# One query against 8192 keys, sixteen heads: another signal for the K loads, fixed transpose addresses, another end

## The chip, the cores and the metric

The kernel runs on one core of a Trainium2 chip. Its metric is the time of one execution on the device, in microseconds, the median over several runs. The core has a matrix engine (TensorE, PE in the profile), three engines for element work (VectorE, DVE; ScalarE, ACT; GpSimd, POOL), a fifth that only issues transfers (SyncE, SP), and 16 DMA engines that bring data from memory to the on-chip buffers. Each engine runs its own instruction list; they meet through counters (semaphores) that one engine raises and another waits for.

## The reference, cut

```python
B, H, Sq, Sk, D = 1, 16, 1, 8192, 256          # q, k, v in bf16

def reference(q, k, v):
    scale = q.shape[-1] ** -0.5
    scores = jnp.einsum("bhqd,bhkd->bhqk", q, k) * scale
    p = _softmax(scores, axis=-1)
    return jnp.einsum("bhqk,bhkd->bhqd", p, v)
```

For each of 16 heads one query row is multiplied with 8192 keys, the scores go through a softmax, and the weights sum up 8192 rows of V. K and V of a head are 4 MB each, so 134 MB are read for 8 KB of output.

## The kernel before

A head's 8192 rows are laid out as 128 partitions of 64 rows each: partition p holds rows 64p to 64p + 63, and "column" j is the j-th row of every partition, 256 numbers in each. `kbuf` and `vbuf` each hold two heads; even heads use the first half, odd heads the second (the parity of the head).

**Loads.** SyncE issues every load in the order of a list, `stream`, built at the top. It begins K0 (in three pieces), K1, the first half of V0, K2, the rest of V0, half of V1, K3, the rest of V1, and then K of head h+2 and V of head h in turn. All go through one queue. Before K of head h (from head 2 on) SyncE waits for the counter `m`, before V of head h for `pr`: the buffer's former user must be done. V of the last two heads is cut into 4 and 9 pieces, and nothing of K comes behind K15. GpSimd waits for each landing and raises `kc` (by eights of columns) or `vc` (by pairs of columns); this is `POOLq L179` and `L181` in the profile.

**Scores.** VectorE computes the first 48 columns of a head, one instruction each (L238: multiply with the query, sum into one column of `S`), in three runs of 16 (`NC` = 3, the loop variable is c); each half run raises `kd` (preset to 2, 6 per head). TensorE computes the last 16 columns: four groups of four columns are transposed into `tp` (`ktrans`, L302, eight transposes a group, each with an address that the engine's sequencer works out from the head), ScalarE copies each group to `KT` (L429), and TensorE multiplies (L316); ScalarE copies the 16 results to `S` and raises `sc`.

**Softmax.** The largest score is found in steps that travel with the next head: four columns into head h+1 VectorE takes the maximum of head h over each partition (`largest`, L214, raises `m`), TensorE transposes that (L284, `mT`), VectorE reduces it after column 16 (`xmax`, L205, raises `g`), TensorE spreads it to all partitions (L288), ScalarE makes the exponentials `E` (even columns in its first half, odd ones in its second) and their sum.

**Values.** TensorE takes V two columns at a time (L374): one matmul of 33 weight columns against 512 numbers, of which row 0 with the first 256 (the even column) and row 32 with the last 256 (the odd column) are used; a head is 32 such pairs after a zeroing matmul (L369). It works on head h-2 while the scores of head h are made: its list for one turn is scores of h, values of h-2, sum of h-1. ScalarE then brings row 32, scaled, to `part` (`other`, L451), and VectorE adds row 0, scaled (`final_of`, L217), into `o_sb`. The last head ends differently: its last eight columns are in a branch of their own, the last four of them go singly into another bank (`TAIL`, L402), and VectorE does two operations, `part` and then `o_sb`. ScalarE then stores all 16 heads, 8 KB in one row (L486).

The counters start from presets, which GpSimd gives at the start from `AHEAD`.

Of the kernel before, what the change touches and what calls it, by code (L numbers as in the profile page):

```python
# [12 lines left out]
GRP = 4  # L13
CH = 8
RUN = 16
PL = 4
ROWS = 33
K_FIRST = (16, 32)
V_SPLIT = {
# [3 lines left out]
    14: (0, 16, 32, 48),  # L23
    15: (0, 16, 32, 40, 48, 52, 56, 60, 62),
}
AHEAD = {"vc": 64, "sc": 1, "sp": 2, "m": 1, "fin": 4, "rc": 3, "l": 2, "qs": 2, "pr": 3, "pt": 3, "kd": 2}


def bass_standalone__mha_softmax__decode_kernel(nc: bass.Bass, q: bass.AP, k: bass.AP, v: bass.AP, out: bass.AP):
# [10 lines left out]
    NC = JD // RUN  # L40
    VU = J // 2
    LAST = H - 1
    TAIL = (LAST + 1) % 2 * 512
    dt = k.dtype


# [27 lines left out]
    with contextlib.ExitStack() as ctx:  # L74
# [60 lines left out]
        for name in ("l", "rc", "pr", "pt", "ps", "pv", "fin", "kd", "ldq", "out"):  # L135
            sem(name)
        for _, _, _, _, name, _ in stream:
            sem(name)
# [4 lines left out]
        @(lambda f: f(nc.sync))  # L143
        def _(sp):
            for kind, h, a, b, name, _ in stream:
                if h >= 2 and a == 0:
                    if kind == "k":
                        sp.wait_ge(sem("m"), h)
                    else:
                        sp.wait_ge(sem("pr"), h + 2)  # L150
                at = (h % 2) * J * D
                sp.dma_start(
                    (kbuf if kind == "k" else vbuf)[:, at + a * D : at + b * D],
                    src(k if kind == "k" else v, h)[:, a * D : b * D],
                ).then_inc(sem(name), 16)
            sp.nop()

        @(lambda f: f(nc.gpsimd))
# [43 lines left out]
        def _(dve):  # L202
# [10 lines left out]
                dve.wait_ge(sem("sc"), h.count(1, 2))  # L213
                dve.tensor_reduce(m[:, :], S[:, ds(h.i * J, J)], AX.X, ALU.max).then_inc(sem("m"), 1)  # L214

            def final(h, bank, to):
                return dve.scalar_tensor_tensor(  # L217
                    out=to,
                    in0=acc[0:1, ds(bank, D)],
                    scalar=recip[0:1, ds(h.i, 1)],  # L220
                    in1=part[0:1, ds(h.i * D, D)],
                    op0=ALU.mult,
                    op1=ALU.add,
                )

            def final_of(h):
                dve.wait_ge(sem("pt"), h.count(1, 4))
                final(h, (h.i % 2) * 512, o_sb[0:1, ds(h.i * D, D)]).then_inc(sem("fin"), 1)

            def turn(h):  # L230
                par = dve.snap(h % 2)
                qh = q_all[:, ds(h * D, D)]
                with dve.Fori(0, NC) as c:
                    dve.wait_ge(sem("kc"), h * KC + c * (RUN // CH) + RUN // CH)
                    for b in range(RUN):
                        if b % (RUN // 2) == 0:
                            dve.wait_ge(sem("kd"), h * (2 * NC) + c * 2 + 1 + b // (RUN // 2))
                        ins = dve.scalar_tensor_tensor(  # L238
                            out=junk[:, b * D : (b + 1) * D],
                            in0=kbuf[:, ds(par * (J * D) + c * (RUN * D) + b * D, D)],  # L240
                            scalar=SCALE,
                            in1=qh,
                            op0=ALU.mult,
                            op1=ALU.mult,
                            accum_out=S[:, ds(h * J + c * RUN + b, 1)],
                        )
                        if b % (RUN // 2) == RUN // 2 - 1:
                            ins.then_inc(sem("kd"), 1)
                        if b == 3:
                            with dve.If(c == 0):  # L250
                                with dve.If(h > 0):
                                    largest(Head(h, 1))
                    with dve.If(c == 0):
                        with dve.If(h > 0):
                            xmax(Head(h, 1))
                    with dve.If(c == 1):  # L256
                        with dve.If(h > 1):
                            recips(Head(h, 2))
                        with dve.If(h > 2):
                            final_of(Head(h, 3))  # L260
                dve.wait_ge(sem("qs"), h // 2 + 4)  # L261

            with dve.Fori(0, 2) as phase:
                with dve.If(phase == 1):
                    dve.wait_ge(sem("qs"), 3)
                    with dve.Fori(0, H) as h:  # L266
                        turn(h)
                    largest(Head(H - 1))
                    recips(Head(H - 2))
                    final_of(Head(H - 3))  # L270
                    xmax(Head(H - 1))
                    recips(Head(H - 1))
                    final_of(Head(H - 2))
                    dve.wait_ge(sem("pt"), H + 3)
                    final(Head(LAST), LAST % 2 * 512, part[0:1, LAST * D : H * D]).then_inc(sem("ps"), 1)
                    dve.wait_ge(sem("ps"), 1)
                    dve.wait_ge(sem("pv"), 1)
                    final(Head(LAST), TAIL, o_sb[0:1, LAST * D : H * D]).then_inc(sem("fin"), 1)

        @(lambda f: f(nc.tensor))  # L280
        def _(pe):
# [14 lines left out]
                    qps[0:ROWS, 0:1], lhsT=lsum[:, 0:1].to_broadcast([P, ROWS]), rhs=ones_col[:, 0:1], start=True, stop=True  # L296
                ).then_inc(sem("l"), 1)

            def ktrans(at, gi):
                for b in range(GRP):  # L300
                    for hf in range(NH):
                        ins = pe.transpose(  # L302
                            tp[gi % 2][:, b * D + hf * P : b * D + (hf + 1) * P],
                            kbuf[:, ds(at + (JD + gi * GRP + b) * D + hf * P, P)],
                            identb[:, :],
                        )
                ins.then_inc(sem("tp"), 1)
# [39 lines left out]
                    ins.then_inc(sem("qp"), 1)  # L347
                pe.wait_ge(sem("cf"), 4)

            def scores(h):  # L350
                now = Head(h)
                at = pe.snap((h % 2) * (J * D))
                pe.wait_ge(sem("kc"), h * KC + KC)
                ktrans(at, 0)
                for gi in range(1, NG):
                    ktrans(at, gi)
                    kscore(now, gi - 1)
                with pe.If(h > 0):
                    transpose_m(Head(h, 1))
                kscore(now, NG - 1)  # L360
                with pe.If(h > 0):
                    bcast(Head(h, 1))

            def values(h):
                o = pe.snap(Head(h, 2).i)
                par = pe.snap(o % 2)
                both = acc[0:ROWS, ds(par * 512, 2 * D)]
                pe.wait_ge(sem("fin"), h + 1)
                pe.matmul(both, lhsT=zero[:, 0:ROWS], rhs=zero[:, :], start=True, stop=False)  # L369

                def pair(j, stop=False):
                    if j % 4 == 0:
                        pe.wait_ge(sem("vc"), h * VU + (j + 4) // 2)
                    return pe.matmul(  # L374
                        both,
                        lhsT=E[:, ds(o * J + j // 2, ROWS)],
                        rhs=vbuf[:, ds(par * (J * D) + j * D, 2 * D)],
                        start=False,
                        stop=stop,
                    )  # L380

                for j in range(0, J - 2 * PL, 2):
# [6 lines left out]
                    pair(j)  # L389
                with pe.If(h < H + 1):  # L390
                    for j in range(J - 2 * PL, J, 2):
                        ins = pair(j, j == J - 2)
                    ins.then_inc(sem("pr"), 1)
                with pe.If(h == H + 1):
                    for j in range(J - 2 * PL, J - PL, 2):
                        ins = pair(j, j == J - PL - 2)
                    ins.then_inc(sem("pr"), 1)
                    pe.wait_ge(sem("fin"), H + 3)
                    for j in range(J - PL, J):
                        if j % 2 == 0:  # L400
                            pe.wait_ge(sem("vc"), (H + 1) * VU + (j + 2) // 2)
                        ins = pe.matmul(  # L402
                            acc[0:1, TAIL : TAIL + D],
                            lhsT=E[:, LAST * J + (j % 2) * (J // 2) + j // 2 :][:, 0:1],
                            rhs=vbuf[:, LAST % 2 * (J * D) + j * D :][:, 0:D],
                            start=j == J - PL,
                            stop=j == J - 1,
                        )
                    ins.then_inc(sem("pv"), 1)

            with pe.Fori(0, 2) as phase:
                with pe.If(phase == 1):
                    with pe.Fori(0, H + 2) as h:
                        with pe.If(h < H):
                            scores(h)
# [8 lines left out]
        @(lambda f: f(nc.scalar))  # L424
        def _(act):
            def evac(h, gi):
                act.wait_ge(sem("tp"), h * NG + gi + 1)
                act.wait_ge(sem("sp"), h * NG + gi + 1)
                act.activation(out=KT[gi % 2][:, :], in_=tp[gi % 2][:, :], func=ACT.Copy).then_inc(sem("kt"), 1)  # L429

# [55 lines left out]
            act.dma_start(out.rearrange("b h s d -> (b s) (h d)"), o_sb[:, :]).then_inc(sem("out"), 16)  # L486
            act.wait_ge(sem("out"), 16)
            act.nop()


# [26 lines left out]
```

## Time and profile before

| | |
|---|---|
| median of 3 runs | 326.32 us (326.3 to 326.52) |
| the profiled execution | 326.13 us |
| its span, first to last instruction | 324.3 us |
| VectorE busy | 281.2 us, 87% |
| TensorE busy | 257.2 us, 79% (granted clock 0.826 in the mean) |
| ScalarE busy | 94.0 us, 29% |
| DMA | 134.27 MB, 414 GB/s over the span |
| SyncE waiting for VectorE's `m` | 256.2 us in 14 waits |

The profile gives busy time by engine, the rate of the transfers by slice, who waited for whom, and single instructions with their start. A row of the timeline reads: start, duration, engine, line, operation, output<-inputs, how many, and in brackets the idle time before it and what ended it. A row of stretches reads: from:to, length, busy time of each engine with the number of instructions, then the TensorE clock that was granted (1.00 is full), the DMA share and GB/s.

### The profile page before, as it was taken

The numbers are of one execution on the slowest core, as the hardware profiler recorded it, in microseconds if no ns is written. First come the engines' busy times: TensorE is split into PE (matmuls) and PEld (weight loads), VectorE is DVE, ScalarE is ACT, GpSimd is POOL, SyncE is SP. The second block draws the span as 40 slices with busy tenths as digits, with TensorE's granted clock in tenths as the row PEclk, the third lists the DMA queues.
The fourth block names the chain that finished last, engine by engine and source line by source line (L and its number), as shares of the span: only waits on it lengthen the run. The fifth ranks groups of instructions, "written<-read, shape, count | busy, mean of one in ns | idle before, by whom it ended". The sixth has DMA issues, their size and how long they took to land. (4 is left out here: it accounts for less than half of the span.)

```text
span 324.3 us, 8901 instructions
## 1 busy us (share of the span) xinstructions
PE 257.2 (79%) x1668; PEld 138.3 (43%) x1668; DVE 281.2 (87%) x1601; ACT 94.0 (29%) x154; POOL 1.8 (1%) x11
## 2 busy tenths in 40 slices
PE   3547259889797978968698796878979698789986
PEld 1235234536353453624446253453624445254442
DVE  0998999999999899898898989889888997988901
ACT  4446040514133060411405033060511405033010
POOL 2000000000000000000000000000000000000000
PEclk9999999969595885959678596966959787595999
DMA  8999999999999999999999999999999999999990
GB/s 312 456 404 384 420 449 424 372 404 453 445 408 441 453 408 432 449 392 453 445 396 453 449 408 436 453 412 428 453 424 416 453 432 408 453 410 415 421 404 33
DMA packets 6949, 134.27 MB, mean 414 GB/s; under 512 B 785, under 2 KB 1057, under 8 KB 1697
## 3 DMA queue, kind: packets, MB, share of 16 engines
q1 hardware_dynamic: 6912, 134.22, 97.1%
q8 instruction: 1, 0.02, 0.0%
q10 hardware_dynamic: 34, 0.02, 0.0%
q14 instruction: 2, 0.02, 0.0%
HBM read 134.23 MB, written 0.01 MB: 414 GB/s over the span
## 5 line engine op out<-in xcount | busy, mean ns | idle before, releaser
L238 DVE SCALAR_TENSOR_TENSOR junk<-kbuf,q_all 128x256 bf16 x768 | 269.9, 416 | 28.3 <-POOLq L179 17.5
L374 PE MATMUL acc<-vbuf,E 128*33 x510 | 142.9, 448 | 18.4 <-POOLq L181 18.3
L374 PEld LDWEIGHTS acc<-vbuf,E 128*33 x510 | 56.8, 112 | 102.6 <-issue 62.6
L302 PE MATMUL tp<-identb,kbuf 128*128 128x128 bf16 x512 | 67.6, 241 | 16.8 <-POOLq L179 16.8
L429 ACT ACTIVATE KT<-tp 128x1024 bf16<-128x1024 bf16 x64 | 65.3, 1023 | 36.1 <-PE tp L302 34.6
L302 PEld LDWEIGHTS tp<-identb,kbuf 128*128 x512 | 48.7, 98 | 30.4 <-issue 17.9
L238 DVE DVE_READ_ACCUMULATOR junk<-kbuf,q_all x768 | 60.4, 79 | 0.0
L451 ACT ACTIVATE part<-acc,recip (+1 forms) x16 | 7.5, 466 | 154.2 <-PE acc L374 154.2
L316 PE MATMUL spe<-q_col,KT 128*128 x512 | 24.8, 167 | 10.4 <-ACT KT L429 10.4
L316 PEld LDWEIGHTS spe<-q_col,KT 128*128 128x128 bf16 x512 | 19.0, 101 | 21.9 <-ACT KT L429 12.6
L288 PE MATMUL sm<-g,ones_row 1*128 (+1 forms) x32 | 9.0, 349 | 9.6 <-DVE g L205 9.0
L288 PEld LDWEIGHTS sm<-g,ones_row 1*128 1x128 f32 x32 | 7.8, 299 | 11.2 <-issue 11.1
L439 ACT ACTIVATE E<-S,negb (+1 forms) x16 | 9.3, 580 | 2.4 <-ACT negb L437 2.4
L369 PE MATMUL acc<-zero 128*33 128x512 bf16 x16 | 9.3, 583 | 0.8 <-issue 0.8
L284 PE MATMUL mx<-ident,m 128*1 128x128 f32 x32 | 8.2, 350 | 0.9 <-DVE m L214 0.9
L437 ACT ACTIVATE negb<-sm 128x1 f32 (+1 forms) x16 | 2.7, 171 | 19.8 <-PE sm L288 19.8
L217 DVE SCALAR_TENSOR_TENSOR o_sb<-acc,recip,part (+1 forms) x16 | 7.3, 455 | 0.4 <-ACT part L451 0.4
L217 DVE SCALAR_TENSOR_TENSOR part<-acc,recip,part 1x256 f32<-1x256 f32 x1 | 0.5, 473 | 7.9 <-ACT part L451 7.9
L209 DVE RECIPROCAL recip<-qps 33x1 f32 (+1 forms) x16 | 2.5, 153 | 5.0 <-PE qps L295 5.0
L340 PE MATMUL acc<-q_sb,identb 16*128 16x256 bf16 x16 | 4.6, 390 | 2.7 <-issue 1.5
L469 ACT ACTIVATE q_all<-acc x8 | 4.8, 597 | 3.1 <-PE acc L340 3.1
L433 ACT ACTIVATE S<-spe 128x16 f32 x16 | 2.9, 183 | 9.4 <-PE spe L316 9.4
(25 smaller groups left out, 29.4 us busy)
## 6 DMA issues: line engine op xcount, KB each, us to landing
kbuf<-in_k_dram SPq DMA_DIRECT2D x15, 4096.0 KB, 17.0
vbuf<-in_v_dram SPq DMA_DIRECT2D x11, 4096.0 KB, 26.3
vbuf<-in_v_dram SPq DMA_DIRECT2D x6, 2048.0 KB, 21.3
vbuf<-in_v_dram SPq DMA_DIRECT2D x6, 1024.0 KB, 13.7
kbuf<-in_k_dram SPq DMA_DIRECT2D x2, 1024.0 KB, 7.0
kbuf<-in_k_dram SPq DMA_DIRECT2D x1, 2048.0 KB, 12.4
vbuf<-in_v_dram SPq DMA_DIRECT2D x2, 512.0 KB, 8.7
vbuf<-in_v_dram SPq DMA_DIRECT2D x3, 256.0 KB, 9.5
```

Of the source, the lines that this page charges most:

```text
L217: return dve.scalar_tensor_tensor(out=to, in0=acc[0:1, ds(bank, D)], scalar=recip[0:1, ds(h.i, 1)], in1=part[0:1, ds(h.i * D, D)], op0=ALU ...
L238: ins = dve.scalar_tensor_tensor(out=junk[:, b * D : (b + 1) * D], in0=kbuf[:, ds(par * (J * D) + c * (RUN * D) + b * D, D)], scalar=SCALE ...
L284: pe.matmul(mx[0:1, 0:P], lhsT=m[:, :], rhs=ident[:, :], start=True, stop=True).then_inc(sem("mT"), 1)
L288: pe.matmul(sm[:, 0:1], lhsT=ones_row[0:1, 0:P], rhs=g[0:1, ds(h.i, 1)], start=True, stop=True).then_inc(sem("bc"), 1)
L302: ins = pe.transpose(tp[gi % 2][:, b * D + hf * P : b * D + (hf + 1) * P], kbuf[:, ds(at + (JD + gi * GRP + b) * D + hf * P, P)], identb[: ...
L316: ins = pe.matmul(spe[:, c : c + 1], lhsT=KT[gi % 2][:, b * D + hf * P : b * D + (hf + 1) * P], rhs=q_col[:, ds(h.i * NH + hf, 1)], start= ...
L369: pe.matmul(both, lhsT=zero[:, 0:ROWS], rhs=zero[:, :], start=True, stop=False)
L374: return pe.matmul(both, lhsT=E[:, ds(o * J + j // 2, ROWS)], rhs=vbuf[:, ds(par * (J * D) + j * D, 2 * D)], start=False, stop=stop,)
L429: act.activation(out=KT[gi % 2][:, :], in_=tp[gi % 2][:, :], func=ACT.Copy).then_inc(sem("kt"), 1)
L439: act.activation(out=E[:, ds(h.i * J, J)].rearrange("p (two x) -> p x two", two=2), in_=S[:, ds(h.i * J, J)].rearrange("p (x two) -> p x t ...
L451: act.activation(out=part[0:1, ds(h.i * D, D)], in_=acc[ROWS - 1 : ROWS, ds((h.i % 2) * 512 + D, D)], func=ACT.Copy, scale=recip[ROWS - 1 ...
L469: act.activation(out=q_all[:, ds(i * (2 * D), 2 * D)], in_=acc[:, ds((i % 2) * 512, 2 * D)], func=ACT.Copy).then_inc(sem("qs"), 1)
```

## The change

Six edits. SyncE's K load waits for `kd` (the 48 columns of VectorE) instead of `m`. Since `kd` says nothing of TensorE's 16 columns, VectorE waits in the ninth column of each run for `tp`, the count of transposed groups, so that a full `kd` means that these are read as well; `tp` gets a preset of 1, and ScalarE's wait for it one more. The transposes are written twice, for even and odd heads, so that their addresses are constants. In every head the last four V columns (`PL` = 4) go singly into row 0 of the same bank, behind the point where ScalarE may fetch row 32; a new count `pv`, 3 ahead, says when they are done, VectorE's `final` and the V loads wait for it, and the last head's own branch goes. `vc` is asked for at nine places of a head instead of every four columns. And the output is stored by SyncE in two pieces: heads 0 to 14, and then the last head's 512 bytes.

```diff
+V_STEPS = (0, 8, 16, 24, 32, 40, 48, 52, 56)
...
-AHEAD = {"vc": 64, "sc": 1, "sp": 2, "m": 1, "fin": 4, "rc": 3, "l": 2, "qs": 2, "pr": 3, "pt": 3, "kd": 2}
+AHEAD = {"vc": 64, "sc": 1, "sp": 2, "m": 1, "fin": 4, "rc": 3, "l": 2, "qs": 2, "pr": 3, "pt": 3, "pv": 3, "kd": 2, "tp": 1}
...
                     if kind == "k":
-                        sp.wait_ge(sem("m"), h)
+                        sp.wait_ge(sem("kd"), (h - 1) * (2 * NC) + 2)
                     else:
-                        sp.wait_ge(sem("pr"), h + 2)
+                        sp.wait_ge(sem("pv"), h + 2)
...
+            heads = out.rearrange("b h s d -> (b s) (h d)")
+            for a, b in ((0, LAST), (LAST, H)):
+                sp.wait_ge(sem("fin"), b + 4)
+                sp.dma_start(heads[:, a * D : b * D], o_sb[:, a * D : b * D]).then_inc(sem("out"), 16)
+            sp.wait_ge(sem("out"), 32)
...
+            def final(h):
+                dve.wait_ge(sem("pt"), h.count(1, 4))
+                dve.wait_ge(sem("pv"), h.count(1, 4))
+                dve.scalar_tensor_tensor(
+                    out=o_sb[0:1, ds(h.i * D, D)],
+                    in0=acc[0:1, ds((h.i % 2) * 512, D)],
...
                         if b % (RUN // 2) == 0:
                             dve.wait_ge(sem("kd"), h * (2 * NC) + c * 2 + 1 + b // (RUN // 2))
+                        if b == RUN // 2:
+                            dve.wait_ge(sem("tp"), h * NG + c * (NG // 2) + 1)
...
-            def ktrans(at, gi):
+            def ktrans(par, gi):
...
-                            kbuf[:, ds(at + (JD + gi * GRP + b) * D + hf * P, P)],
+                            kbuf[:, par * (J * D) + (JD + gi * GRP + b) * D + hf * P :][:, 0:P],
...
+                for j in range(J - PL, J):
+                    if j % 2 == 0:
+                        pe.wait_ge(sem("vc"), h * VU + (j + 2) // 2)
+                    ins = pe.matmul(
+                        acc[0:1, ds(par * 512, D)],
+                        lhsT=E[:, ds(o * J + (j % 2) * (J // 2) + j // 2, 1)],
+                        rhs=vbuf[:, ds(par * (J * D) + j * D, D)],
+                        start=False,
+                        stop=j == J - 1,
+                        skip_group_check=True,
+                    )
+                ins.then_inc(sem("pv"), 1)
...
+                            pe.wait_ge(sem("kc"), h * KC + KC)
+                            with pe.If(h % 2 == 0):
+                                scores(h, 0)
+                            with pe.If(h % 2 == 1):
+                                scores(h, 1)
...
-                act.wait_ge(sem("tp"), h * NG + gi + 1)
+                act.wait_ge(sem("tp"), h * NG + gi + 2)
...
-            act.wait_ge(sem("fin"), H + 4)
-            act.dma_start(out.rearrange("b h s d -> (b s) (h d)"), o_sb[:, :]).then_inc(sem("out"), 16)
-            act.wait_ge(sem("out"), 16)
```

TensorE at the start of a head's scores, before (`ISA` and `REGISTER_ALU` are address and counter steps of the engine's sequencer; in brackets what a row waits for):

```order
L353 ISA
L302 ISA [waits kc]
L302 MATMUL tp<-identb,kbuf 128x128
L302 ISA
L302 MATMUL tp<-identb,kbuf 128x128
```

Now, for an even head:

```order
L399 ISA
L400 REGISTER_ALU [waits kc]
L400 COMPARE_AND_BRANCH
L303 MATMUL tp<-identb,kbuf 128x128 x16
L311 ISA
L313 REGISTER_ALU [waits kt]
```

The address step ahead of each transpose is gone, and sixteen transposes follow each other; a branch on the parity stands ahead of them.

VectorE in the middle of a run of sixteen columns, before:

```order
L238 SCALAR_TENSOR_TENSOR junk,S<-kbuf,q_all 128x256
L237 REGISTER_ALU
L238 ISA [waits kd]
L238 SCALAR_TENSOR_TENSOR junk,S<-kbuf,q_all 128x256
L238 ISA
```

Now:

```order
L243 SCALAR_TENSOR_TENSOR junk,S<-kbuf,q_all 128x256
L240 REGISTER_ALU
L242 ISA [waits kd]
L243 ISA [waits tp]
L243 SCALAR_TENSOR_TENSOR junk,S<-kbuf,q_all 128x256
```

The wait for the transposes stands in front of the ninth column, and all later columns of the head behind it.

TensorE at the end of the last head's values, before, from the branch of its own on:

```order
L394 COMPARE_AND_BRANCH
L373 REGISTER_ALU
L374 ISA [waits vc]
L374 MATMUL acc<-vbuf,E 33x512
L374 ISA
L374 MATMUL acc<-vbuf,E 33x512
L402 MATMUL acc<-vbuf,E 1x256 [waits vc,fin]
L402 MATMUL acc<-vbuf,E 1x256
L402 MATMUL acc<-vbuf,E 1x256 [waits vc]
L402 MATMUL acc<-vbuf,E 1x256
```

Now, for every head:

```order
L374 ISA [waits vc]
L374 MATMUL acc<-vbuf,E 33x512
L374 ISA
L374 MATMUL acc<-vbuf,E 33x512
L384 REGISTER_ALU
L385 ISA [waits vc]
L385 MATMUL acc<-vbuf,E 1x256
L385 ISA
L385 MATMUL acc<-vbuf,E 1x256
L384 REGISTER_ALU
L385 ISA [waits vc]
L385 MATMUL acc<-vbuf,E 1x256
```

The branch is gone, the singles stand in every head's list, each with an address step, and no longer wait for `fin`.

More of the change, by code (lines that the diff above doesn't have):

```diff
@@ L223, in final @@
                     op1=ALU.add,
[L224 to L228, printed above, removed]
+                ).then_inc(sem("fin"), 1)
             def turn(h):
@@ L269, in _ @@
                     recips(Head(H - 2))
-                    final_of(Head(H - 3))
+                    final(Head(H - 3))
                     xmax(Head(H - 1))
                     recips(Head(H - 1))
[L273 to L278, printed above, removed]
+                    final(Head(H - 2))
+                    final(Head(LAST))
         @(lambda f: f(nc.tensor))
@@ L348, in spread, with scores @@
                 pe.wait_ge(sem("cf"), 4)
[L350 removed]
+            def scores(h, par):
                 now = Head(h)
[L352 to L354 removed]
+                ktrans(par, 0)
                 for gi in range(1, NG):
[L356 removed]
+                    ktrans(par, gi)
                     kscore(now, gi - 1)
[L358 to L362, printed above, removed]
             def values(h):
@@ L366, in values @@
                 par = pe.snap(o % 2)
+                pe.wait_ge(sem("fin"), h + 1)
                 both = acc[0:ROWS, ds(par * 512, 2 * D)]
-                pe.wait_ge(sem("fin"), h + 1)
                 pe.matmul(both, lhsT=zero[:, 0:ROWS], rhs=zero[:, :], start=True, stop=False)
[L371 to L382, printed above, removed]
+                for j in range(0, J - PL, 2):
                     if j == 20:
@@ L388, in values @@
                             bcast(Head(H - 1))
[L389 to L409, printed above, removed]
+                    if j in V_STEPS:
+                        units = (V_STEPS + (J - PL,))[V_STEPS.index(j) + 1] // 2
+                        pe.wait_ge(sem("vc"), h * VU + units)
+                    ins = pe.matmul(
+                        both,
+                        lhsT=E[:, ds(o * J + j // 2, ROWS)],
+                        rhs=vbuf[:, ds(par * (J * D) + j * D, 2 * D)],
+                        start=False,
+                        stop=j == J - PL - 2,
+                    )
+                ins.then_inc(sem("pr"), 1)
+                for j in range(J - PL, J):
+                    if j % 2 == 0:
+                        pe.wait_ge(sem("vc"), h * VU + (j + 2) // 2)
+                    ins = pe.matmul(
+                        acc[0:1, ds(par * 512, D)],
+                        lhsT=E[:, ds(o * J + (j % 2) * (J // 2) + j // 2, 1)],
+                        rhs=vbuf[:, ds(par * (J * D) + j * D, D)],
+                        start=False,
+                        stop=j == J - 1,
+                        skip_group_check=True,
+                    )
+                ins.then_inc(sem("pv"), 1)
             with pe.Fori(0, 2) as phase:
```

15 lines of the change are left out of this document (7 added, 8 removed).

## The prediction

> **What bounds the kernel now.** I read the page first, for which engine is full and whether the transfers ever pause; then the stretches of the transfer rate, to find where; then SyncE's waits, to find what holds a load back; then the tail in order of time.
>
> ```profile
> span 324.3 us, 8901 instructions
> ...
> DMA  8999999999999999999999999999999999999990
> GB/s 312 456 404 384 420 449 424 372 404 453 445 408 441 453 408 432 449 392 453 445 396 453 449 408 436 453 412 428 453 424 416 453 432 408 453 410 415 421 404 33
> ```
>
> The DMA row stands at 9 from the second slice to the last but one. So the loads are the bound: 134 MB go through one pipe, and what isn't saved in that pipe, or behind its end, is saved nowhere. The slices are too coarse to show a pause, so I asked for longer stretches. The last three columns are the TensorE clock, the DMA share and GB/s.
>
> ```profile
> 24.00:34.00 10.00, 6.88 (x70) 5.09 (x70) 8.49 (x49) 5.03 (x8) 0.00 (x0) 1.00 0.97 388
> 34.00:58.00 24.00, 15.06 (x99) 8.49 (x100) 23.91 (x140) 5.03 (x8) 0.00 (x0) 1.00 1.00 430
> 58.00:90.00 32.00, 27.27 (x196) 15.39 (x195) 31.80 (x183) 10.78 (x18) 0.00 (x0) 0.79 0.98 413
> 61.70:62.70 1.00, 1.00 (x16) 0.85 (x15) 1.00 (x8) 0.36 (x1) 0.00 (x0) 1.00 0.13 33
> 90.00:288.00 198.00, 165.76 (x1049) 87.99 (x1046) 180.41 (x1030) 55.32 (x91) 0.00 (x0) 0.77 1.00 431
> ```
>
> From 90 on the pipe gives 431 GB/s without a break, and that is its speed. It falls short in two places only. In 24 to 34 it loses (431 - 388) / 431 x 10 = 1.00 us, in 58 to 90 (431 - 413) / 431 x 32 = 1.34 us; the microsecond after 61.70 moved 33 GB/s, which is a queue that has run dry. Together 2.3 us: all that earlier loads can win, since a full pipe takes nothing more.
>
> ```profile
> SPq L152 <- DVE m L214: 256.2, 14, 22.9
> SPq L152 <- PE acc L374: 30.8, 2, 15.4
> ```
> ```profile
> 26.20 0.33 SPq L152 DMA_DIRECT2D kbuf<-in_k_dram  x1
> 61.74 0.33 SPq L152 DMA_DIRECT2D kbuf<-in_k_dram  x1
> ```
>
> The two pauses sit at the issue of K of head 2 (26.20) and of head 4 (61.74). SyncE waited for m, which VectorE makes four columns into the next head, and both rows show that it issues at once when m is there.
>
> **The change, part by part.**
>
> *K loads wait for VectorE's column counter.* VectorE's rows for heads 0 and 2: the last column's read, then m.
>
> ```profile
> 24.11 0.08 DVE L238 DVE_READ_ACCUMULATOR junk<-kbuf,q_all  x1
> 25.95 0.22 DVE L214 TENSOR_REDUCE m<-S 128x1 f32 x1
> 59.93 0.08 DVE L238 DVE_READ_ACCUMULATOR junk<-kbuf,q_all  x1
> 61.50 0.21 DVE L214 TENSOR_REDUCE m<-S 128x1 f32 x1
> ```
>
> The counter is full at 24.19 and 60.01, m came at 26.17 and 61.71: the loads can go 2.0 and 1.7 us sooner, if VectorE's pace stays. From the issue at 61.74 to full flow about a microsecond passes (the 33 GB/s), so K must be issued 1.0 us before the queue is dry. First pause: dry at about 26.6 (26.20 to 27.20 still moved part of its bytes), K issued at 24.2, flow from 25.2: 1.4 us in hand. Closed, 1.0 us won. Second pause: the stream then ends 1.0 sooner, at 60.8 in place of about 61.8, so K of head 4 must be issued by 59.8, and the counter as before gives 60.0. This is the close call, and VectorE's pace in heads 0 and 1 decides it.
>
> *The new wait on the transposes.* What SyncE no longer asks, VectorE now asks in its column 24 (two groups transposed) and column 40 (all four). Queued behind that wait are its own columns, and SyncE behind those.
>
> ```profile
> 14.30 2.24 PE L302 MATMUL tp<-identb,kbuf 128*128 128x128 bf16 x16 [2.93 <-POOLq L179]
> 15.79 0.42 DVE L238 SCALAR_TENSOR_TENSOR junk<-kbuf,q_all 128x256 bf16 x1
> 24.01 2.21 PE L302 MATMUL tp<-identb,kbuf 128*128 128x128 bf16 x16 [3.10 <-POOLq L179]
> 29.38 0.59 PE L284 MATMUL mx<-ident,m 128*1 128x128 f32 x2
> 31.63 0.43 DVE L238 SCALAR_TENSOR_TENSOR junk<-kbuf,q_all 128x256 bf16 x1 [1.13 <-issue]
> ```
> ```profile
> L238 DVE SCALAR_TENSOR_TENSOR junk<-kbuf,q_all 128x256 bf16 x768 | 269.9, 416 | 28.3 <-POOLq L179 17.5
> ...
> L429 ACT ACTIVATE KT<-tp 128x1024 bf16<-128x1024 bf16 x64 | 65.3, 1023 | 36.1 <-PE tp L302 34.6
> ```
>
> In head 0 K lands in three pieces, VectorE starts with the first and TensorE with the last, so column 24 begins at 15.79 and the first sixteen transposes end at 16.54: a stall of at most 16.54 - 15.79 plus some 0.4 to start again, 1.1 us, and at least nothing. The fixed addresses shorten the sixteen. They come at 0.14 us each with an address instruction before each; the four single matmuls at the end of the program, with fixed addresses, come at 0.15 with 256 columns and a start (their row is below), 0.11 in sequence. I take 0.09 for 128 columns, so 1.4 us instead of 2.2, 0.2 for the new parity branch: ready at 16.0, stall 0.6. In later heads K lands whole and both engines start together: two groups are done 2.2 us in (the row at 24.01), VectorE is at column 24 after 24 x 0.35 = 8.4 (269.9 / 768); nothing there.
>
> *The transposes with fixed addresses* give back more than that. From the first transpose to mx (24.01 to 29.38) 5.4 us pass; with the transposes short, ScalarE's three copies of 1.02 us set it, and mx comes about 1.1 sooner. VectorE's g waits for mx, and the 1.13 us idle before 31.63 is VectorE's sequencer starting again after that wait. Gone, if mx is 1 us sooner. Net over heads 0 and 1: +0.6 - 1.1 = -0.5, so head 2 ends at 59.5, K of head 4 is issued at 59.6, against the 59.8 needed. Closed by 0.2: I count 2.2 of the 2.3.
>
> ```profile
> DVE junk L238 <- POOLq L179: 10.0, 10, 1.2
> DVE junk L238 <- issue: 8.0, 9, 1.0
> PE acc L374 <- POOLq L181: 17.5, 9, 2.0
> ```
>
> Between 110 and 290 (these rows) VectorE waits 1.0 us a head for K to land and TensorE 1.9 us a head for V: what is added there is covered. So V's wait for pv in place of pr, the four single matmuls and the longer queue are worth nothing in the middle. If that cover were gone (2 us a head), TensorE would be late next. On SyncE's queue the V load stands behind K's and waits for head h-2's values; at the two pauses no V wait stands ahead of the K load.
>
> *The tail.* In order of time:
>
> ```profile
> 295.37 0.43 DVE L238 SCALAR_TENSOR_TENSOR junk<-kbuf,q_all 128x256 bf16 x1 [0.99 <-issue]
> ...
> 307.27 0.38 PE L284 MATMUL mx<-ident,m 128*1 128x128 f32 x2 [0.40 <-DVE m L214]
> ...
> 309.29 3.63 PE L374 MATMUL acc<-vbuf,E 128*33 x16
> ...
> 314.05 7.25 PE L374 MATMUL acc<-vbuf,E 128*33 x30
> ...
> 320.69 0.24 PEld L374 LDWEIGHTS acc<-vbuf,E 128*33 x2 [0.55 <-issue]
> ...
> 321.23 0.60 PE L402 MATMUL acc<-vbuf,E 128*1 128x256 bf16 x4
> 321.39 0.47 ACT L451 ACTIVATE part<-acc,recip 1x256 f32<-1x256 f32 x1 [7.91 <-PE acc L374]
> 321.89 0.47 DVE L217 SCALAR_TENSOR_TENSOR part<-acc,recip,part 1x256 f32<-1x256 f32 x1 [7.91 <-ACT part L451]
> 322.40 0.47 DVE L217 SCALAR_TENSOR_TENSOR o_sb<-acc,recip,part 1x256 bf16<-1x256 f32 x1
> 322.90 0.48 ACTq L486 DMA_DIRECT2D out_dram<-o_sb  x1
> ```
>
> In these rows TensorE waits for m, never for V, so what is taken off this chain counts in full. One VectorE operation instead of two: 322.40 - 321.89 = 0.51. The branch before the last eight columns (0.55 idle on the weight loads, less the 0.23 that a pair takes anyway, 3.63 / 16): about 0.3. The wait for m, 0.40, since VectorE in head 15 also loses its 0.99 restart. The singles: 4 x 0.11 against two pairs of 0.23 is even on the array, and their address instructions cost at most 0.14 - 0.11 = 0.03 each, 0.12 a head: 0.2 back for heads 13 and 14; in head 15 they run beside ScalarE's 0.47. The store: no row shows a 512-byte one. From below nothing, from above 0.15 (0.48 against SyncE's 0.33 to issue) plus 0.30 (8 KB on one of 16 engines, 431 / 16 = 27 GB/s); as one engine carries the row now, I take 0.3. The idle between head 14 and 15 I leave. Tail: 0.51 + 0.3 + 0.40 - 0.2 + 0.3 = 1.3 us, between 0.5 and 2.0.
>
> [...]
>
> Sum: the profiled execution took 326.13 us, 1.83 more than its span; 326.13 - 2.2 - 1.3 = 322.6. The median of the runs is 0.19 above that execution: **322.8 us**.
>
> **The rivals.**
>
> *A, the second pause stays.* The stall in head 0 is the full 1.1 and head 1 gives nothing back: head 2 ends at 61.1, K of head 4 flows 1.3 us late, and the second pause keeps nearly its 1.34. For it: a margin of 0.2 on three estimates. Against it: the 1.13 in head 1 is a restart, and even an unchanged mx would be less late when VectorE is. Time: 326.3 - 1.0 - 0.1 - 1.3 = 323.9.
>
> *B, the pauses cost nothing in the end.* The stream is won but the tail waits for something else, say head 15's columns at VectorE's pace. For it: the chain of the tail is not on a load. Against it: VectorE waits a microsecond for K in ten heads, so it follows the stream. Time: 326.3 - 1.3 = 325.0.
>
> *C, half clock in the tail: slower.* TensorE's granted clock with the pairs of the V stage:
>
> ```profile
> 295.40:299.35 3.95, 3.92 (x10) 1.46 (x10) 0.50 0.97 407
> 299.35:304.30 4.95, 4.95 (x24) 2.12 (x22) 1.00 1.02 424
> ```
>
> A pair takes 3.92 / 10 = 0.39 us at half clock and 4.95 / 24 = 0.21 at full. After 299.35 the tail runs at full clock; between 90 and 288 the mean is 0.77, half clock for 46% of the time. If the last 27 us got that share, 12.4 us would be at half clock and lose (0.39 - 0.21) / 0.39 of it, 5.7 us: 322.8 + 5.7 = 328.5. It turns to slower from 9 us at half clock (4.1 us lost). [...]
>
> **How the numbers follow.** Forecast 0.60, A 0.18, B 0.08, C 0.05, the rest 0.09 (most of it a tail that wins more or less than its bounds). Low end: the whole 2.3 and a tail of 2.0 or a little more, 321.8; high end: A with a tail of 0.5, 324.7, which leaves B and C outside. The runs of before spread over 0.07%, so 0.2% (0.65 us) is about what can be told from no change; forecast, A and B are all beyond it. Faster 0.89, same 0.05, slower 0.06.
>
> **What would show it.** Right: no microsecond between 24 and 90 below 400 GB/s; K of head 2 issued near 24.8 and of head 4 near 59.6; no idle before the first column of a second run; one VectorE operation after ScalarE's last. Wrong: a drop of the rate near 61, VectorE idle at column 24 of head 0 by more than a microsecond, half clock after 300, or TensorE's transposes still at 0.14 us.

## The result, and the profile after

The changed kernel takes 323.83 us in the median of 5 runs (323.79 to 324.61), the kernel before 326.37: a ratio of 0.9925, 95% interval 0.9907 to 0.9942. It is 2.5 us faster, and the forecast was 3.5. The time lies inside the range, but by luck: the sum behind it does not hold. The stream of loads, for which 2.2 us were counted, gave nothing that is left at the end, and the tail, for which 1.3 us were counted, gave nearly all.

The page after, its busy times and its transfers:

```profile
span 322.5 us, 8531 instructions
...
PE 232.7 (72%) x1698; PEld 122.6 (38%) x1698; DVE 281.4 (87%) x1600; ACT 91.0 (28%) x154; POOL 1.8 (1%) x11
...
DMA packets 6951, 134.27 MB, mean 416 GB/s; under 512 B 786, under 2 KB 1059, under 8 KB 1700
```

The span is 1.8 us shorter. The profiled execution took 323.79 us, so 1.3 lie outside the span, and before it was 1.8: another half microsecond, which no engine's row shows.

The same stretches as before, of the changed kernel (GB/s is the last column):

```profile
24.00:34.00 10.00, 6.44 (x70) 5.19 (x70) 9.75 (x57) 4.92 (x8) 0.00 (x0) 1.00 1.01 413
34.00:58.00 24.00, 14.23 (x97) 8.25 (x96) 23.91 (x140) 4.92 (x8) 0.00 (x0) 1.00 0.98 423
58.00:90.00 32.00, 25.46 (x200) 13.64 (x198) 31.80 (x184) 10.56 (x18) 0.00 (x0) 0.79 1.00 424
```

By these rates the stream looks better at both pauses, 388 to 413 and 413 to 424, 0.6 and 0.8 us at 431 GB/s. The drop near 61 us that the prediction named as a sign of being wrong is still there:

```profile
62.00:63.00 1.00, 1.00 (x28) 1.00 (x27) 1.00 (x7) 0.70 (x2) 0.00 (x0) 1.00 0.53 180
```

Now the landing of what was issued, the page's transfer lines, the first of before and the second of after (the last column is the median time from issue to landing):

```profile
kbuf<-in_k_dram SPq DMA_DIRECT2D x15, 4096.0 KB, 17.0
```
```profile
kbuf<-in_k_dram SPq DMA_DIRECT2D x15, 4096.0 KB, 20.2
```

The K loads are issued some 3 us sooner (that of head 15 at 267.45 in place of 270.65) and take 3.2 us longer. They stand in the queue for what they won. TensorE's first transposes of head 15, which need its K, are not earlier either; first before, then after:

```profile
287.89 1.79 PE L302 MATMUL tp<-identb,kbuf 128*128 128x128 bf16 x13 [0.59 <-POOLq L179]
```
```profile
288.28 0.89 PE L303 MATMUL tp<-identb,kbuf 128*128 128x128 bf16 x13 [0.18 <-issue]
```

Before, the row waits for the landing. After, TensorE comes to it 0.6 us behind the landing, since it has the sum of an earlier head to end first (at 288.09). By the landing records K of head 15 is there at 287.65 us before and at 287.70 after. From that landing to the end it is 36.7 us before and 34.8 after: the whole gain of the span is in this piece. In order of time:

```profile
305.37 2.32 PE L374 MATMUL acc<-vbuf,E 128*33 x10
307.62 0.38 PE L285 MATMUL mx<-ident,m 128*1 128x128 f32 x2
...
309.63 3.20 PE L374 MATMUL acc<-vbuf,E 128*33 x14
312.76 0.60 PE L385 MATMUL acc<-vbuf,E 128*1 x4
...
313.37 0.38 PE L363 MATMUL acc<-zero 128*33 128x512 bf16 x1
313.59 6.64 PE L374 MATMUL acc<-vbuf,E 128*33 x30
...
320.86 0.47 DVE L224 SCALAR_TENSOR_TENSOR o_sb<-acc,recip,part 1x256 bf16<-1x256 f32 x1 [6.74 <-ACT part L444]
321.36 0.25 SPq L159 DMA_DIRECT2D out_dram<-o_sb  x1
```

No row of TensorE here has a bracket: it waits for nothing. Head 15's pairs begin at 313.59 (before 314.05), take 6.64 us (7.25), and one VectorE operation stands between them and the store.

### The profile page after: what moved, and what is told of

Read it like the earlier page. It is cut to its first block, busy times and chain, and to the rows that moved or that the text cites. A ratio compares the mean times of both kernels' runs of the same rounds, so it can differ in the third digit from the quotient of the medians.

```text
span 322.5 us, 8531 instructions
## 1 busy us (share of the span) xinstructions
PE 232.7 (72%) x1698; PEld 122.6 (38%) x1698; DVE 281.4 (87%) x1600; ACT 91.0 (28%) x154; POOL 1.8 (1%) x11
## 5 line engine op out<-in xcount | busy, mean ns | idle before, releaser
L374 PE MATMUL acc<-vbuf,E 128*33 x480 | 136.2, 452 | 18.6 <-POOLq L186 18.6
L374 PEld LDWEIGHTS acc<-vbuf,E 128*33 x480 | 54.1, 113 | 98.2 <-issue 61.3
L422 ACT ACTIVATE KT<-tp 128x1024 bf16<-128x1024 bf16 x64 | 62.3, 1021 | 33.6 <-PE tp L303 33.4
L243 DVE DVE_READ_ACCUMULATOR junk<-kbuf,q_all x768 | 61.9, 81 | 0.0
L303 PE MATMUL tp<-identb,kbuf 128*128 128x128 bf16 x512 | 41.3, 236 | 17.3 <-POOLq L184 17.0
L303 PEld LDWEIGHTS tp<-identb,kbuf 128*128 128x128 bf16 x512 | 33.0, 106 | 18.5 <-issue 18.4
L317 PEld LDWEIGHTS spe<-q_col,KT 128*128 128x128 bf16 x512 | 20.5, 99 | 36.0 <-issue 25.7
L385 PE MATMUL acc<-vbuf,E 128*1 x64 | 9.6, 272 | 0.0
L285 PE MATMUL mx<-ident,m 128*1 128x128 f32 x32 | 6.7, 294 | 1.6 <-issue 0.9
L385 PEld LDWEIGHTS acc<-vbuf,E 128*1 x64 | 4.0, 82 | 7.6 <-issue 6.8
```

The lines of the kernel that those rows point to most:

```text
L243: ins = dve.scalar_tensor_tensor(out=junk[:, b * D : (b + 1) * D], in0=kbuf[:, ds(par * (J * D) + c * (RUN * D) + b * D, D)], scalar=SCALE ...
L285: pe.matmul(mx[0:1, 0:P], lhsT=m[:, :], rhs=ident[:, :], start=True, stop=True).then_inc(sem("mT"), 1)
L303: ins = pe.transpose(tp[gi % 2][:, b * D + hf * P : b * D + (hf + 1) * P], kbuf[:, par * (J * D) + (JD + gi * GRP + b) * D + hf * P :][:, ...
L317: ins = pe.matmul(spe[:, c : c + 1], lhsT=KT[gi % 2][:, b * D + hf * P : b * D + (hf + 1) * P], rhs=q_col[:, ds(h.i * NH + hf, 1)], start= ...
L374: ins = pe.matmul(both, lhsT=E[:, ds(o * J + j // 2, ROWS)], rhs=vbuf[:, ds(par * (J * D) + j * D, 2 * D)], start=False, stop=j == J - PL - 2,
L385: ins = pe.matmul(acc[0:1, ds(par * 512, D)], lhsT=E[:, ds(o * J + (j % 2) * (J // 2) + j // 2, 1)], rhs=vbuf[:, ds(par * (J * D) + j * D, ...
```

## The experiments

Two theories stood against each other. **S**: a landing counts when the last of the 16 DMA engines has its share, so a pause costs only what it adds for the engine that is last behind it; the K wait moved almost none of it, and the gain is the tail and the store. **R**, the prediction's: the mean rate counts, and the earlier K loads won their part. Twelve kernels, each timed against the kernel before on the same chip; runs of one kernel spread by 0.6 to 1.3 us (three by 2.2 to 2.6), so differences under 0.5 us in the medians are not read. Landings and rows are those of one profiled execution of each kernel.

**The changed kernel again**, as the measure.

> The changed kernel itself, as the measure for the others on this chip. Both theories: 323.8 us, as measured. Theory S (the slowest of the 16 DMA engines sets every landing; the stream won nothing and the gain of 2.5 us is the tail and the end): K of head 15 lands at 287.7 us as in the kernel before. Theory R (the earlier K loads won about a microsecond of stream, the rest is the tail) expects the same total here; the next run tells them apart.

323.17 us, ratio 0.9917 (0.9904 to 0.9930). K of head 15 landed at 287.47.

**The K wait undone:**

```diff
-                        sp.wait_ge(sem("kd"), (h - 1) * (2 * NC) + 2)
+                        sp.wait_ge(sem("m"), h)
...
-                        if b == RUN // 2:
-                            dve.wait_ge(sem("tp"), h * NG + c * (NG // 2) + 1)
```

> The changed kernel, but the K loads wait for m again and VectorE no longer waits for the transposes. S: the K wait gave nothing, so the time stays at 323.8 us, at most 0.4 off either way (head 0 of VectorE loses its stall of 1.4 us, while the second pause comes back by 0.35). R: the pause at 61 us comes back in full and the time rises by 1 to 2 us, to 324.8 to 325.8.

323.68 us, 0.9927 (0.9915 to 0.9940), K of head 15 at 287.79. Half a microsecond, or nothing: the interval lies within that of the changed kernel's first runs (0.9907 to 0.9942). R's 1 to 2 us are out.

**The K wait alone**, put into the kernel before (`kd` for SyncE, `tp` for VectorE, nothing else).

> The kernel before with nothing but the first edit: K loads wait for VectorE's columns, VectorE waits for the transposes, which keep their sequencer addresses. Prediction, without the fixed addresses: 1.0 to 1.3 us faster than before. Theory S: K of head 15 lands within 0.4 us of 287.6 as before, and the time is within 0.4 us of the kernel before.

326.13 us over 12 runs, 0.9987 (0.9964 to 1.0010): no change that can be told. The interval reaches 1.2 us on the faster side, so the times alone do not rule out the prediction's 1.0; the landing does, with K of head 15 at 287.68 against 287.65. SyncE's issue of K of head 4 and the end of the wait for K of head 15 in its trace:

```profile
60.16 0.33 SPq L152 DMA_DIRECT2D kbuf<-in_k_dram  x1
```
```profile
287.91 1.26 PE L304 MATMUL tp<-identb,kbuf 128*128 128x128 bf16 x9 [0.87 <-POOLq L179]
```

Issued at 60.16 in place of 61.74, and head 15 begins at 287.91 in place of 287.89. The edit does what it says, and nothing moves at the end.

**No pause at all.** K of heads 2 to 5 in two pieces, the first (columns 0 to 31) as soon as VectorE has done two runs:

```diff
+            load("k", h, 0, 32, f"k{h % 2}")
+            load("k", h, 32, J, f"k{h % 2}_e")
...
-                        sp.wait_ge(sem("kd"), (h - 1) * (2 * NC) + 2)
+                        sp.wait_ge(sem("kd"), (h - 1) * (2 * NC) + 2 - (2 if b == 32 else 0))
```

> The changed kernel, but K of heads 2 to 5 is loaded in two pieces, and the first (columns 0 to 31) waits only for the first two runs of VectorE, about 6 us sooner. So every DMA engine has work at both pauses. Theory S (a load must be issued some 2.7 us before the last engine is dry; the pause at 62 us costs the last engine 1.0 us, the one at 27 us next to nothing): K of head 15 lands about 1.1 us sooner, at 286.4, and the time is 1.0 to 1.3 us under the changed kernel. Prediction (mean rate of the engines: 0.4 us still lost at the first pause, 0.5 to 1.0 at the second): 0.9 to 1.9 us under. If the pauses cost nothing in the end, 0.

322.66 us, 0.9883 (0.9869 to 0.9898); K of head 15 landed at 286.59, 1.1 us sooner. This is what the pauses had to give, about half of the 2.3 that were counted, and what the change didn't win. The size fits S and lies in R's range too, so the next run had to part them.

**Only K of head 4 in two pieces**; the pause at 27 us stays, the one at 62 goes.

> The changed kernel with only K of head 4 in two pieces, the first of them early. Theory S (the last engine has a backlog at the pause of 27 us and never idles there; only the pause at 62 us costs): the whole gain of the kernel with four early K loads, about 1.1 us under the changed kernel, K of head 15 landing at 286.4 to 286.8. Prediction (mean rate): the first pause's part of about half stays lost, 0.5 us under the changed kernel.

322.32 us, 0.9885 (0.9871 to 0.9900). Its stretches and the start of head 15:

```profile
24.00:34.00 10.00, 6.50 (x70) 5.19 (x70) 9.74 (x57) 4.92 (x8) 0.00 (x0) 1.00 0.97 403
34.00:58.00 24.00, 14.44 (x94) 8.25 (x95) 23.91 (x140) 4.92 (x8) 0.00 (x0) 1.00 0.99 427
58.00:90.00 32.00, 26.06 (x199) 13.86 (x198) 31.71 (x183) 10.56 (x18) 0.00 (x0) 0.79 1.01 435
```
```profile
287.28 1.06 PE L311 MATMUL tp<-identb,kbuf 128*128 128x128 bf16 x16 [1.08 <-POOLq L192]
```

K of head 15 landed at 286.71. At the first pause the rate is poor, 403 GB/s against 413 in the changed kernel, and yet nearly the whole gain is there: 1.0 to 1.3 us by the ratios, where the mean rate gave 0.5. By that rate this pause takes (431 - 403) / 431 x 10 = 0.65 us. Counted by landings, as is done below, it took 0.4 here, and nothing in the kernel before, where the rate is 388. So the price does not follow the rate: the change raised it there and won nothing, and this run left it low and lost less than it says.

**The same with the new VectorE wait asked for once a head**, in column 40, on top of the four early K loads.

> As the run with K of heads 2 to 5 in two pieces, and VectorE asks for the transposes only once a head, in column 40, which is enough for a full count to mean that they are done. Theory S: with the queue never dry, the 1.4 us that head 0 of VectorE loses are covered, so nothing is added: within 0.3 us of the run before. If VectorE's pace in the first heads counts, up to 1 us faster.

322.23 us, 0.9884 (0.9869 to 0.9898), K of head 15 at 286.43. The same as without (322.66, 286.59): in these two kernels VectorE's delay in head 0 is covered. This kernel and the two above beat the changed one; of the three the one with K of head 4 alone needs the least.

**The transposes with sequencer addresses again**, all else as changed.

> The changed kernel, but the transposes get their addresses from the sequencer again, in one list for both parities. Prediction: VectorE's restart of about a microsecond after g comes back in every head, m of head 15 is late and TensorE waits for it again: 0.4 to 1.0 us slower than the changed kernel. Theory S: from 294 us on the chain is TensorE alone, which in the changed kernel reaches the transpose of m a microsecond after m is there, so the restart is covered: 0 to 0.3 us slower.

324.13 us, 0.9944 (0.9931 to 0.9957): slower by 0.2 to 0.3%, 0.6 to 0.9 us (0.4 to 0.8 by the medians), more than S allowed and as the prediction had it. VectorE's restarts, before, changed, and this one (the rows of waits, with total, number and longest):

```profile
DVE junk L238 <- issue: 10.5, 12, 1.1
```
```profile
DVE junk L243 <- issue: 2.9, 12, 0.4
```
```profile
DVE junk L243 <- issue: 10.8, 12, 1.2
```

The mechanism is as predicted: short transposes take away the restart after g. But in this trace TensorE reaches the transpose of m at 307.63 with m there since 307.22, as late as in the changed kernel (307.62), so the trace doesn't show how the restart would get to the end. Its size stays open: the medians of the changed kernel itself lie 0.7 us apart (323.83 and 323.17), TensorE's clock (below) makes 0.5 in one stage (10.1 and 9.6 us), and in this execution the two pauses cost 0.6 us more than in the changed kernel (table below).

**The new V stage alone**, in the kernel before (singles, no branch, one final operation, nine waits).

> The kernel before with the new V stage alone: the last four V columns singly in every head, no branch for the last head, one VectorE operation at the end, V asked for at nine places; K loads, transpose addresses and the store as before. Theory S: K of head 15 lands as before, and the end after it is 1.4 to 1.9 us shorter than before's 36.7: 324.4 to 324.9 where the kernel before takes 326.3. Prediction's own terms for this part (0.51 + 0.3 - 0.2): 0.6 us faster.

325.12 us, 0.9965 (0.9953 to 0.9977): 1.1 us, between the two expectations. K of head 15 lands at 287.92 here, and from there to the end it is 35.3 us, 1.4 less than before. TensorE between head 14 and head 15:

```profile
313.36 0.22 PE L289 MATMUL qps<-ones_col,lsum 128*33 128x1 f32 x2
313.64 0.39 PE L358 MATMUL acc<-zero 128*33 128x512 bf16 x1
314.01 6.65 PE L369 MATMUL acc<-vbuf,E 128*33 x30
```

Before, 0.81 us idle stood between the two first rows, and the pairs took 7.25. So the idle time goes with the V stage's new code, of which the branch is a part.

**V asked for every four columns**, all else as changed.

```diff
-V_STEPS = (0, 8, 16, 24, 32, 40, 48, 52, 56)
+V_STEPS = tuple(range(0, 60, 4))
```

> The changed kernel, but TensorE asks for the landed V columns every four columns again, 15 times a head in place of 9. If the missing counter steps are why the 0.8 us idle between heads 14 and 15 and the gaps inside head 15's pairs went away, 0.8 to 1.4 us come back: 324.6 to 325.2. If the missing branch of the last head is why, it stays within 0.2 of 323.8.

323.59 us, 0.9925 (0.9913 to 0.9938). The idle time between the heads does not come back: the last sum starts at 312.22 and head 15 at 312.47. So it was not the number of waits; the pairs of head 15 take 7.04 us in place of 6.64, so the waits are worth 0.4 there. What is left is the missing branch or the singles, and no run parts these two. The sequencer's records show how the gap closes. The turn of TensorE's loop takes its sequencer 0.8 us in both kernels, 312.67 to 313.46 before and 312.16 to 312.95 in the changed one. Before, TensorE has only the short sum left (to 312.96) and runs out of work; in the changed kernel it still has pairs and singles to do, to 313.36, and the turn is hidden behind them.

**The store**: by ScalarE in one row (all else as changed), then alone in the kernel before, then by SyncE in one row.

> The changed kernel, but all 16 heads are stored by ScalarE in one row of 8 KB at the end, as before. If the short store by SyncE was worth what the two traces show (1.40 us from issue to end against 1.14, and 0.5 us less outside the span), the time rises by 0.26 to 0.8 us, to 324.1 to 324.6. If a store costs the same whatever its size and queue, it stays at 323.8.

> The kernel before with the new store alone: heads 0 to 14, then 512 bytes, by SyncE. Theory S: 0.3 us in the span and 0.5 us behind it, 0.8 us faster than before. Prediction's term: 0.3 us. [...]

> The changed kernel, but SyncE stores all 8 KB in one row at the end. If the size makes the 0.3 us in the span, they come back and the half microsecond behind the span does not: 0.2 to 0.4 us slower than the changed kernel. If the issuing engine makes both, it is as fast as the changed kernel.

The first took 323.90 us (0.9932; 0.9915 to 0.9950), the second 325.53 (0.9981; 0.9973 to 0.9990), the third 324.33 (0.9936; 0.9915 to 0.9956). The medians alone say little for the first and the third, whose runs spread over 2 us; the second is clear, 0.6 us faster than before, between the prediction's 0.3 and S's 0.8. The profiled executions part the two effects:

| stored by | from the store's issue to the end of the span | outside the span |
|---|---|---|
| ScalarE, 8 KB (before, first) | 1.4, 1.4 us | 1.8, 1.9 us |
| SyncE, last piece 512 B (changed, second) | 1.1, 1.1 us | 1.3, 1.3 us |
| SyncE, 8 KB (third) | 1.4 us | 1.4 us |

with, for the third, the row of the store:

```profile
321.52 0.32 SPq L159 DMA_DIRECT2D out_dram<-o_sb  x1
```

The size makes the 0.3 us in the span: by the packet records the 8 KB go as one packet of 0.31 us and the 512 bytes as one of 0.03. The 0.5 us behind the span go with the engine that issues the last store and waits for it; why, no record shows.

## Why the prediction came out as it did

**Where the queue pauses, and that K's issue sets it: right.** K of head 4 was issued at 60.47 in place of 61.74 (59.6 forecast), K of head 2 at 25.88 in place of 26.20 (24.8 forecast; most of the rest went into the stall in head 0, below).

**The price of the pauses: wrong, the step that failed.** The prediction took a mean rate, 388 and 413 GB/s against 431, for lost time, 1.00 and 1.34 us. It is a mean over 16 engines, and they don't run level. By the packet records of the changed kernel the first engine had its share of K of head 1 at 21.8 us and the last at 23.6. When the queue runs out near 27 us, the early engines idle until there is new work, and the late one is still at the old: in the kernel before the first has ended that V piece at 26.58, and no packet of K of head 2 starts before 27.17, while the last ends it at 28.20, and a packet of K follows at 28.21. So the first pause is idle time of engines that are ahead. The landings show it too. Each load leaves 16 landing records, and the kernel waits for all 16; of the V piece ahead of that pause they run from 27.02 to 28.65, 1.6 us, of K of head 2 behind it from 37.90 to 38.37. Against the 9.71 us of a full queue (below) 1.2 us were lost between the first landings, between the last ones nothing.

At the second pause the last landing does come later. In the kernel before, all engines had run dry: the last packet of V ends at 62.31, and the first of K starts at 62.69. In the changed kernel the engine that was last with V runs on without a break, at 62.74, but another gets its first packet of K only at 63.15, and now that one lands last (read off the times of the packets; the records name no engine). The price of a pause is the distance from the last landing of the V piece before it to that of K of head 2 or 4, less 9.71 us, the distance between two 4 MB landings when the queue is full (V of head 12 to K of head 15):

| kernel | K of head 4 issued | price of the first pause | of the second | K of head 15 landed | span |
|---|---|---|---|---|---|
| before | 61.74 | 0.0 | 1.40 | 287.65 | 324.3 |
| K wait alone | 60.16 | 0.0 | 1.56 | 287.68 | 324.4 |
| K wait undone | 61.98 | 0.0 | 1.49 | 287.79 | 322.1 |
| changed | 60.47 | 0.0 | 1.05 | 287.70 | 322.5 |
| changed, again | 60.38 | 0.0 | 0.97 | 287.47 | 321.8 |
| changed, V every four columns | 60.21 | 0.7 | 0.21 | 287.03 | 322.0 |
| changed, sequencer addresses | 60.20 | 0.5 | 1.06 | 287.76 | 322.6 |
| K of head 4 in two pieces | 54.53 | 0.4 | 0.1 | 286.71 | 320.9 |
| K of heads 2 to 5 in two pieces | 54.57 | 0.1 | 0.1 | 286.59 | 321.3 |

Both prices together are 1.4 to 1.5 us in the four kernels whose K loads wait for m, and 0.9 to 2.0 us, 1.4 in the mean, in the seven whose whole K loads wait for `kd`. So the K wait won nothing on average; it made the price uneven. And the first pause is not always free: it took 0.1 to 0.7 us in four of these seven and 0.4 with K of head 4 in two pieces.

**The time from issue to flow: wrong, 1.0 us.** That was read off the mean rate again, and it is the first engine's. In the changed kernel, K of head 4 is issued at 60.47, its first packet starts at 61.48, but the last of the 16 engines starts its first one at 63.15, 2.7 us after the issue, and 14 of the 16 first packets, of 32 KB, take 1.6 to 2.1 us where later ones take 1.21. By these figures the margin would have had to be near 3 us, not 1, and the load came too late for that at 59.6 as at 60.5. That is an estimate: no run has such a margin, and K of head 4 in two pieces has some 7 us. With the same gate the price of the second pause varied from 0.2 to 1.6 us between kernels; what decides it was not settled.

**The stall in head 0: too small.** 0.6 us were taken, with 1.1 as the upper end; it was 1.4. VectorE's rows at column 24 and at the next run's first column:

```profile
16.71 0.42 DVE L243 SCALAR_TENSOR_TENSOR junk<-kbuf,q_all 128x256 bf16 x1 [0.57 <-PE tp L303]
```
```profile
20.23 0.43 DVE L243 SCALAR_TENSOR_TENSOR junk<-kbuf,q_all 128x256 bf16 x1 [0.67 <-DVE junk L243]
```

The first is the wait as told. The second is the sequencer: its counter and address steps for the next turn of the loop run from 19.51 to 20.18 while VectorE idles. That it had lost its lead at the wait is our reading. The sixteen transposes took 1.88 us there, not 1.4. The prediction names no row for the 0.2 of the parity branch, nor for the 0.4 of VectorE's start; the runs show this: from the landing of K's last piece to the first transpose it is 0.24 us before (14.06 to 14.30) and 0.31 with the branch (14.34 to 14.65), and column 24 begins 0.18 us behind the last transpose (16.53 and 16.71). Later heads took no harm (VectorE waits for the transposes once in the whole execution, 0.6 us), and the restart in head 1 went as forecast (1.13 us became 0.16).

**The tail: right in kind, too small, and differently made up.** Forecast 1.3 us, measured 1.8 in the span and 0.5 behind it. One VectorE operation for two: 0.51 forecast; from the last pair's end to VectorE's end 1.57 us became 1.10, so 0.47. The branch: 0.3 forecast; the pairs of head 15 got 0.6 shorter, but two thirds of that are the fewer waits, for which the prediction had no term. The idle time between the heads, "left" as it is: 0.8 gained, the largest term. The wait for m: gone, as forecast, but TensorE comes there at 307.62 and not sooner than before's 307.27, so nothing of its 0.40 was won: the values of head 13 took 10.1 us in place of 9.3 (305.15 - 295.08 against 304.34 - 295.03). A part of that is the four singles. Another is the clock, which in the changed kernel's two profiled executions did not rise at the same time; first the one above, then the repetition:

```profile
299.50:302.00 2.50, 2.50 (x11) 0.98 (x9) 0.80 1.02 423
```
```profile
299.50:302.00 2.50, 2.50 (x14) 1.09 (x12) 1.00 1.02 426
```

The half clock lasted to 300.5 us in the first and to 299.3 in the repetition. In the repetition that stage took 9.6 us, and over all kernels of this study it ran from 8.9 to 10.1. The store: 0.3 forecast and 0.3 found in the span, and 0.5 behind it that no term held. In the span that makes 0.47 + 0.61 + 0.81 + 0.3, less 0.35 for the later start at the transpose of m: 1.84, as measured.

**The rivals.** A's second pause did stay, but its time, 323.9 us, is near the measured one by luck: A still counted 1.0 us for the first pause, which gave nothing, and 1.3 for the tail, which gave 2.3. C did not occur: from 300.5 us on the granted clock is full. What lowers it was not shown: in the kernel before it falls to half twelve times from 70 us on, while TensorE never idles longer than 2.0 us, and at 98.0 and 118.4 us with no idle time over 0.3 us in the 7 us ahead. B had the tail independent of the stream; the runs with early K loads show the opposite, about 1 us sooner in the stream (K of head 15 at 286.59 and 286.71 in place of 287.70) and as much at the end (1.0 to 1.3 us by the ratios).

## What to carry to other kernels

The transfer rate is a mean over 16 engines. In the kernel before, the rates priced the two pauses at 1.0 and 1.3 us, the landings at 0.0 and 1.4; with K of head 4 in two pieces they gave 0.65 for the first and the landings 0.4. So price a pause by the distance between landings, not by lost GB/s. To close one, issue the load so early that every engine still has work when its first packet comes, by the estimate above some 3 us ahead in this kernel. A piece of the load on an earlier count (issued at 54.53 in place of 60.47) brought the last K load in 1.0 us sooner; a signal that came 1.3 us sooner brought nothing. Once the loads set the pace, look for gain behind the last load that heads a chain: here the 1.8 us of the span came from there, out of waits, a turn of a loop and small operations, where TensorE waits for nothing else.

## What the runs showed of the hardware that was not expected

The time outside the span depends on which engine issues the last store and waits for it: 1.8 to 1.9 us with ScalarE (four kernels), 1.3 to 1.4 with SyncE (ten kernels, one of them with 8 KB). The first packet of K of head 4, 4 MB into a queue that was running dry, started 1.0 us after the issue on the first engine; on the last it started after 2.0 (before: 61.74, 62.69, 63.73) and 2.7 (changed: 60.47, 61.48, 63.15). And in head 15 a transpose whose address is a constant follows the last one after 0.07 us (the sixteen in 1.06 us above), where one with an address step takes 0.14; in heads 0 and 1 the constant ones took 0.12, and why is open.
